# FFN weights in two halves, the residual loaded into place, VectorE memsets: one change to an S4 and GEGLU kernel, predicted and measured

## The chip, the cores and the metric

The kernel runs on one core of one Trainium2 chip. The metric is the device time of one execution in microseconds (us). "Faster" or "slower" needs 2%. The intervals are 95% intervals of the ratio to the kernel before, measured in the same rounds on the same chip.

Engine names as in the profile: PE is TensorE (PEld its weight loads), DVE is VectorE, ACT is ScalarE, POOL is GpSimd, SP is SyncE. "SPq" and "ACTq" are transfers issued by those engines, and an engine works through its instructions in order. The granted clock of a stretch is the share of TensorE's full clock that the throttle allowed in it. L90 is line 90 of the kernel; the change moves line numbers by a few, so L708 before and L705 after are the same statement.

## The reference, cut to what matters

```python
# u: [1, 2048, 448] bf16; N = 256 states per channel; F = 1792
K = einsum("dn,dnl,dn->dl", C, exp(dt * A * l), dt * B).real       # S4 convolution kernel
y = irfft(rfft(pad(K)) * rfft(pad(layernorm(x))))[:L] + layernorm(x) * Dskip
h  = x + y                                                          # x is the residual
h2 = h + (gelu(ln(h) @ w_gate) * (ln(h) @ w_up)) @ w_down           # the FFN
# outputs: h2 and the gradients of h2 for all twelve inputs (vjp with grad_out)
```

## The kernel before

One core computes forward and backward. These stages matter here, in order of time: the kernel K is generated and its lags are expanded (`expand_lags`, to 393 us); K is transformed (`dft_forward`, to 452); the product is transformed back and becomes h (`dft_inverse`, to 530); the FFN forward and backward (550 to 829); the transform of the gradient (to 892); a second inverse for dK (to 946); the binning of dK into lags (`bin_lags`, to 978); a third inverse for the input's gradient (to 1038); a last phase over the states.

Names in the code and the profiles: a slice is one pass `kt` of the loop below, and the variants (var) are sums, negatives and differences of input tiles that its matmuls read. Kh, Kx and Kperm are K as loaded, reordered and expanded, and pxl is the expansion's PSUM tile. Uk is a slice of the input's spectrum, xn the normalised input, hn the normalised h, goT the transposed output gradient. Rb and blo are the one-hot and the result tiles of the binning, Mn and Mb the lag tables, DY what the third inverse transforms. A ring is a set of buffers used in turn.

The forward transform, with its variants all built at the start:

```python
var = [work.tile([P, 3, D], BF16, name="var%d" % i) for i in range(8)]
for rho in range(4):
    for jj in range(2):
        s1, s2 = sig[4 * rho + jj], sig[4 * rho + jj + 2]
        nc.vector.tensor_tensor(out=V(rho, jj, 0), in0=s1, in1=s2, op=ALU.add)
        nc.scalar.mul(out=V(rho, jj, 2), in_=s2, mul=-1.0)
for rho in range(4):
    for jj in range(2):
        nc.vector.tensor_tensor(out=V(rho, jj, 1), ..., op=ALU.subtract)
# ... (mid rows)
for kt in range(8):
    # 4 groups of matmuls into PSUM tiles pgrp (a ring of 7)
    on_kt(kt, groups)       # VectorE: butterflies into X, product with Uk into Z[kt]
```

After it, the weights and then the residual, all on SyncE's queue:

```python
self.ffn_weights()          # Wg, Wu (8 loads), WdT (4 transposes), Wd, WgT and WuT (28 transposes)

def consume(tp, pp, pm, scale):            # per tile of the inverse
    x = tmp.tile([P, D], BF16, name="x_t")
    xn = tmp.tile([P, D], BF16, name="xn_t")
    nc.sync.dma_start(out=x[:], in_=tok_rows_ap(self.aps["A_u"][0], tp))
    nc.sync.dma_start(out=xn[:], in_=self.xn_dram[:, tp, :])
    # xn *= Dskip; x += xn; y from PSUM; h_sb[:, tp] = x + y
```

The lag tables and the binning:

```python
nc.gpsimd.memset(self.Mn[:], 0.0)                    # rs_open: 128 x 11200 bf16
nc.gpsimd.memset(t[:], 0.0)                          # Mb, twice 128 x 3200
# bin_lags, for b in range(6): one-hot tiles Rb on VectorE, matmuls into pbl,
# blo[:, 0] by VectorE and blo[:, 1] by ScalarE (a ring of two buffers), then
self.dq().dma_start(out=self.dKl_dram[:][...], in_=o[0:n, :, :])
# rs_load: 40 loads Mn <- dKl_scr, three of four on SyncE, the fourth on ScalarE
```

## Time and profile before

| | us |
|---|---|
| time, median of 3 runs (range) | 1419.27 (1416.28 to 1423.09) |
| span of the profiled run | 1417.6 |
| Kperm complete (end of the expansion) | 393.5 |
| last product of the kernel transform | 451.6 |
| end of the first inverse | 529.6 |
| gate matmuls (ps_g) at full rate | 549.8 |
| end of the second inverse; first DY matmul of the third | 945.7; 977.6 |

The averages of the whole span say little here. In the profile TensorE and VectorE are busy 76% and 79% of the time, but in different stages. The useful question for each stage is which wait ends last in it.

### The profile page before, as it was taken

How to read it: one execution, taken by the hardware profiler on the slowest of the kernel's cores; microseconds unless marked ns; L12 is line 12 of the kernel's file. 1: busy time of each engine (PE TensorE's matmuls, PEld its weight loads, DVE VectorE, ACT ScalarE, POOL GpSimd, SP SyncE). 2: the span in 40 equal slices, each digit the busy share in tenths (PEclk: the TensorE clock that was granted, in tenths of full speed). 3: DMA queues.
4: the chain of work that ended last, by engine and by line, in shares of the span. 5: the costliest groups of instructions: out<-in, count | busy, mean ns of one | idle time of the engine just before them, and what ended most of it. 6: DMA issues, size and time to landing. Idle time of an engine off the chain costs nothing.

```text
span 1417.6 us, 21047 instructions
## 1 busy us (share of the span) xinstructions
PE 1082.5 (76%) x7284; PEld 684.3 (48%) x7284; DVE 1120.4 (79%) x2999; ACT 643.5 (45%) x1110; POOL 275.0 (19%) x378
## 2 busy tenths in 40 slices
PE   0363677877786746999999977877969899779874
PEld 0143355555343325776777633433436555566553
DVE  5889879778798047999999969975796786686785
ACT  3574776858431014665666631111425634552450
POOL 2933544010101000111111120031110221220221
PEclk9855566767998978999999989897989999979986
DMA  5033243343664742344443272225359977988940
GB/s 143 33 134 124 77 181 154 135 163 119 229 216 154 166 117 56 100 114 112 114 113 100 85 242 72 79 56 128 111 126 192 223 165 163 192 176 191 211 82 6
DMA packets 320120, 189.76 MB, mean 134 GB/s; under 512 B 268809, under 2 KB 291661, under 8 KB 319885
## 3 DMA queue, kind: packets, MB, share of 16 engines
q1 hardware_dynamic: 302224, 143.50, 39.1%
q0 software_dynamic: 13696, 42.45, 9.5%
q10 hardware_dynamic: 4092, 2.47, 0.7%
q8 instruction: 57, 0.93, 0.3%
q14 instruction: 51, 0.41, 0.1%
HBM read 44.98 MB, written 83.22 MB: 90 GB/s over the span
## 4 chain that ended last, share of the span: by engine, by line
PE 30%; DVE 19%; DMA 8%; issue 6%; SPq 5%; ACT 3%; POOL 1%; ACTq 0%; DVEq 0%; POOLq 0%
PE ps_o L90 7%; PE pinv L90 5%; PE pw L90 3%; DMA TTr<-T_scr 3%; DMA out_dram<-emit_o 3%; PE pim L1225 3%; PE pre L1225 3%; PE ps_g L90 2%; PE ps_u L90 2%; PE ps_d L90 2%; PE pc L1205 2%; DVE e_t L826 1%; SPq L796 1%; SPq L797 1%; PE pgrp L90 1%
## 5 line engine op out<-in xcount | busy, mean ns | idle before, releaser
L90 PE MATMUL pw<-rowsT,act_b 128*128 128x512 bf16 (+1 forms) x512 | 125.4, 363 | 2.4 <-DMA rowsT<-dG_scr 1.7
L1183 DVE TENSOR_TENSOR u<-C,tb_Z 128x1280 bf16<-128x1280 bf16 x140 | 104.5, 819 | 22.1 <-ACT C L1208 20.8
L1208 ACT CAST C<-pc 128x400 bf16<-128x400 f32 x224 | 102.5, 493 | 39.4 <-PE pc L1205 37.6
L90 PE MATMUL kb<-Pt,T 128*128 128x50 bf16 x896 | 86.0, 264 | 22.5 <-DVE Pt L470 16.6
L90 PEld LDWEIGHTS <-TS 128*128 128x128 bf16 x576 | 57.2, 99 | 92.3 <-issue 42.5
L1205 PE MATMUL pc<-Mb,TTr 128*128 128x100 bf16 x896 | 86.2, 226 | 19.8 <-DMA TTr<-T_scr 8.1
L90 PEld LDWEIGHTS <-TC 128*128 128x128 bf16 x576 | 57.6, 100 | 88.2 <-issue 39.2
L1205 PEld LDWEIGHTS <-TTr 128*128 128x128 bf16 x896 | 66.6, 108 | 68.6 <-issue 42.3
L90 PEld LDWEIGHTS <-T 128*128 128x128 bf16 x896 | 79.5, 122 | 37.5 <-issue 21.3
L606 PE MATMUL pa<-Rq,hl_a 128*128 128x256 bf16 x224 | 43.6, 338 | 59.9 <-DVE Rq L586 46.3
L606 PE MATMUL pa<-Rq,hl_b 128*128 128x256 bf16 x224 | 50.9, 370 | 47.6 <-ACT Cs L648 45.7
L647 ACT ACTIVATE Sn<-pa 128x1024 bf16<-128x1024 f32 x56 | 57.5, 1026 | 49.1 <-DVE T L652 34.8
L90 PEld LDWEIGHTS <-act_b 128*128 128x128 bf16 x512 | 49.4, 100 | 38.6 <-issue 7.6
L90 PE MATMUL ps_d<-goT,WdT 128*128 128x256 bf16 x448 | 61.7, 281 | 6.7 <-DVE ln_v L250 4.7
L606 PEld LDWEIGHTS <-hl_a 128*128 128x128 bf16 x224 | 26.2, 118 | 82.2 <-issue 49.7
L90 PE MATMUL pinv<-Zf,TS 128*128 128x448 bf16 x128 | 45.0, 373 | 26.5 <-DVE ybf L767 26.5
L90 PE MATMUL ps_g<-hnT,Wg 128*128 128x256 bf16 x448 | 60.0, 277 | 6.2 <-DMA hnT<-hn_scr 6.0
L648 ACT ACTIVATE Cs<-pa,halfpi_col 128x1024 bf16<-128x1024 f32 x56 | 62.5, 1117 | 3.0 <-DVE T L653 2.8
L90 PE MATMUL ps_u<-hnT,Wu 128*128 128x256 bf16 x448 | 60.5, 278 | 2.9 <-ACT e_up L864 2.9
L606 PEld LDWEIGHTS <-hl_b 128*128 128x128 bf16 x224 | 27.2, 125 | 72.1 <-issue 64.0
L1225 PEld LDWEIGHTS <-ident 128*128 128x128 bf16 x525 | 52.3, 100 | 18.6 <-issue 7.5
L1256 POOL DMA_DIRECT2D out_dram<-emit_o x84 | 43.9, 529 | 75.9 <-ACT emit_o L1254 72.1
(297 smaller groups left out, 2962.8 us busy)
## 6 DMA issues: line engine op xcount, KB each, us to landing
T_scr<-T SPq DMA_DIRECT2D x56, 512.0 KB
Uk<-U_scr SPq DMA_DIRECT2D x16, 448.0 KB
aT_scr<-f_a POOLq DMA_DIRECT2D x8, 896.0 KB, 6.2
dG_scr<-f_dG POOLq DMA_DIRECT2D x8, 896.0 KB, 7.9
dU_scr<-f_dU POOLq DMA_DIRECT2D x8, 896.0 KB, 9.9
TC<-tab_scr SPq DMA_DIRECT2D x16, 256.0 KB
TS<-tab_scr SPq DMA_DIRECT2D x16, 256.0 KB
U_scr<-X SPq DMA_DIRECT2D x8, 448.0 KB
```

The costliest lines, as they stand in the source:

```text
L90: self.nc.tensor.matmul(out_ap, lhsT=lhsT, rhs=rhs, start=(i == 0), stop=(i == n - 1))
L606: nc.tensor.matmul(pa[:, 2 * h:2 * h + 2, nh, :], lhsT=self.hl[nm][:, blk, nh * 128:(nh + 1) * 128], rhs=Rqf[:, c0:c0 + 256].rearrange("p ...
L647: nc.scalar.activation(out=flat(Sn), in_=flat(pb), func=ACT.Sin)
L648: nc.scalar.activation(out=flat(Cs), in_=flat(pb), func=ACT.Sin, bias=self.halfpi_col[:], scale=-1.0)
L796: nc.sync.dma_start_transpose(out=WgT[:, ft, :], in_=aps["B_w_gate"][:, ft * P:(ft + 1) * P])
L797: nc.sync.dma_start_transpose(out=WuT[:, ft, :], in_=aps["B_w_up"][:, ft * P:(ft + 1) * P])
L826: TT = lambda o, x, y, op: nc.vector.tensor_tensor(out=o[:], in0=x[:], in1=y[:], op=op)
L1183: TT = lambda o, x, y, op: nc.vector.tensor_tensor(out=o, in0=x, in1=y, op=op)
L1205: nc.tensor.matmul(pc[:, k, :, :].rearrange("p r x -> p (r x)"), lhsT=tt[:, k0 + k, c, nh, :], rhs=mv[:, t0 + k0 + k, :], start=True, stop ...
L1208: nc.scalar.copy(out=C[:, c, :, nh, x0:x0 + 8].rearrange("n x (m r) -> n x m r", r=2), in_=pc[:].rearrange("n m r x -> n x m r"))
L1225: nc.tensor.matmul(dst[:], lhsT=wt[:], rhs=prods[i][:, o, :, :].rearrange("p w n -> p (w n)"), start=(o0 == 0 and o == 0 and i in (0, 2)), ...
L1256: nc.gpsimd.dma_start(out=outs[idx][blk * 64:(blk + 1) * 64, nh * P:(nh + 1) * P], in_=ob[nh * 64:(nh + 1) * 64, :])
```

## The change

Its intent is to let the first inverse run without waiting. One half of the weights is loaded during the kernel transform. The residual goes straight into its final tile h_sb, early and on another queue. To make room in SBUF the variants of the transform are built in three groups, two buffers deep, and the ring of Uk and X has two buffers instead of three. In the lag binning GpSimd is freed of its memsets.

```diff
-            var = [work.tile([P, 3, D], ...)]                       # all variants at the start
+            for kts, which in (((0, 1), 0), ((2, 3, 6, 7), 2), ((4, 5), 1)):
+                var = [work.tile([P, D], BF16, name="var%d" % i) for i in range(8)]   # bufs=2
+                ...                                                 # build this group's variants only
+                for kt in kts: ...
@@ forward_conv
+            for tp in range(NT):
+                nc.scalar.dma_start(out=self.h_sb[:, tp, :], in_=tok_rows_ap(self.aps["A_u"][0], tp))
+            self.ffn_open()
...
-                ring = ...(name="fc_ring2", bufs=3)
+                ring = ...(name="fc_ring2", bufs=2)
...
+                    if kt in (2, 3, 4):
+                        self.ffn_weights_first(kt - 2)              # Wg, Wu, WdT
...
-            self.ffn_weights()
+            self.ffn_weights_rest()                                 # Wd, WgT, WuT
             def consume(tp, pp, pm, scale):
-                x = tmp.tile(...); nc.sync.dma_start(out=x[:], ...)
+                x = self.h_sb[:, tp, :]
-                nc.sync.dma_start(out=xn[:], in_=self.xn_dram[:, tp, :])
+                nc.scalar.dma_start(out=xn[:], in_=self.xn_dram[:, tp, :])
@@ bin_lags, rs_open, rs_load
-                self.dq().dma_start(out=self.dKl_dram...)
+                nc.gpsimd.dma_start(out=self.dKl_dram...)
-        nc.gpsimd.memset(self.Mn[:], 0.0)            # and Mb
+        nc.vector.memset(self.Mn[:], 0.0)            # and Mb
-                self.dq(alt=True).dma_start(out=tab, in_=src)
+                (nc.gpsimd if k % 2 else nc.scalar).dma_start(out=tab, in_=src)
```

(The tiles Kh and lag_t of the expansion move to smaller rings; the weight loads are the same but for their order.)

More of the change, by code (lines that the diff above doesn't have):

```diff
@@ L123, in dft_forward @@
         with ExitStack() as es:
-            work = es.enter_context(self.tc.tile_pool(name="dftf_work", bufs=1))
+            work = es.enter_context(self.tc.tile_pool(name="dftf_work", bufs=2))
             psA = es.enter_context(self.tc.tile_pool(name="dftf_psA", bufs=7, space=bass.MemoryType.PSUM))
             psB = es.enter_context(self.tc.tile_pool(name="dftf_psB", bufs=1, space=bass.MemoryType.PSUM))
-            var = [work.tile([P, 3, D], BF16, name="var%d" % i) for i in range(8)]
-            def V(rho, jj, which):
-                return var[2 * rho + jj][:, which, :]
@@ L132, in dft_forward @@
-            for rho in range(4):
-                for jj in range(2):
-                    s1 = sig[4 * rho + jj]
-                    s2 = sig[4 * rho + jj + 2]
-                    nc.vector.tensor_tensor(out=V(rho, jj, 0), in0=s1, in1=s2, op=ALU.add)
-                    nc.scalar.mul(out=V(rho, jj, 2), in_=s2, mul=-1.0)
-            for rho in range(4):
-                for jj in range(2):
-                    nc.vector.tensor_tensor(out=V(rho, jj, 1), in0=sig[4 * rho + jj], in1=sig[4 * rho + jj + 2], op=ALU.subtract)
@@ L142, in dft_forward @@
-            for comp, (rp, rn) in enumerate(((0, 2), (1, 3))):
-                pm = psB.tile([P, D], F32, name="pmid")
-                self.mm_group(pm[:], [(self.ones[:], V(rp, jj, 0)) for jj in range(2)]
-                              + [(self.neg_ones[:], V(rn, jj, 0)) for jj in range(2)])
-                nc.scalar.copy(out=mid[:, comp, :], in_=pm[0:1, :])
-            for kt in range(8):
-                groups = {}
-                for comp in (0, 1):
-                    for par in (0, 1):
-                        pairs = self.dft_pairs(kt, comp, par, self.TC[kt], self.TS[kt], sig, V)
-                        pt = psA.tile([P, D], F32, name="pgrp")
-                        self.mm_group(pt[:], pairs)
-                        groups[(par, comp)] = pt
-                on_kt(kt, groups)
+            for kts, which in (((0, 1), 0), ((2, 3, 6, 7), 2), ((4, 5), 1)):
+                var = [work.tile([P, D], BF16, name="var%d" % i) for i in range(8)]
+                for rho in range(4):
+                    for jj in range(2):
+                        v = var[2 * rho + jj]
+                        s1, s2 = sig[4 * rho + jj], sig[4 * rho + jj + 2]
+                        if which == 2:
+                            nc.scalar.mul(out=v[:], in_=s2, mul=-1.0)
+                        else:
+                            nc.vector.tensor_tensor(out=v[:], in0=s1, in1=s2, op=ALU.add if which == 0 else ALU.subtract)
+                if which == 0:
+                    for comp, (rp, rn) in enumerate(((0, 2), (1, 3))):
+                        pm = psB.tile([P, D], F32, name="pmid")
+                        self.mm_group(pm[:], [(self.ones[:], var[2 * rp + jj][:]) for jj in range(2)]
+                                      + [(self.neg_ones[:], var[2 * rn + jj][:]) for jj in range(2)])
+                        nc.scalar.copy(out=mid[:, comp, :], in_=pm[0:1, :])
+                for kt in kts:
+                    groups = {}
+                    for comp in (0, 1):
+                        for par in (0, 1):
+                            pairs = self.dft_pairs(kt, comp, par, self.TC[kt], self.TS[kt], sig, lambda rho, jj, w: var[2 * rho + jj][:])
+                            pt = psA.tile([P, D], F32, name="pgrp")
+                            self.mm_group(pt[:], pairs)
+                            groups[(par, comp)] = pt
+                    on_kt(kt, groups)
@@ L687, in expand_lags @@
             lag_row = w.tile([P, NT, P], BF16, name="lag_row")
-            t = w.tile([P, 4, 4, P], F32, name="lag_t")
-            nc.gpsimd.iota(t[:], pattern=[[1, 4], [512, 4], [4, P]], base=0, channel_multiplier=0,
-                           allow_small_or_imprecise_dtypes=True)
-            nc.vector.tensor_copy(out=lag_row[:], in_=t[:].rearrange("p r j l -> p (r j) l"))
+            for r in range(4):
+                t = rp.tile([P, 4, P], F32, name="lag_t", bufs=2)
+                nc.gpsimd.iota(t[:], pattern=[[512, 4], [4, P]], base=r, channel_multiplier=0,
+                               allow_small_or_imprecise_dtypes=True)
+                nc.vector.tensor_copy(out=lag_row[:, 4 * r:4 * r + 4, :], in_=t[:])
             Kx = w.tile([P, 6, D], BF16, name="Kx")
-            Kh = w.tile([P, 6, D], BF16, name="Kh")
-            nc.gpsimd.memset(Kh[:, 5, :], 0.0)
             for b in range(6):
                 n = 1 if b == 5 else P
-                self.dq().dma_start(out=Kh[0:n, b, :], in_=Kt_dram[:][b * 128:b * 128 + n, :])
-                nc.scalar.copy(out=Kx[:, b, :].rearrange("p (x r) -> p x r", r=2), in_=Kh[:, b, :].rearrange("p (r x) -> p x r", r=2))
+                Kh = rp.tile([P, D], BF16, name="Kh", bufs=3)
+                if b == 5:
+                    nc.gpsimd.memset(Kh[:], 0.0)
+                self.dq().dma_start(out=Kh[0:n, :], in_=Kt_dram[:][b * 128:b * 128 + n, :])
+                nc.scalar.copy(out=Kx[:, b, :].rearrange("p (x r) -> p x r", r=2), in_=Kh[:].rearrange("p (r x) -> p x r", r=2))
             for tp in range(NT):
@@ L732, in forward_conv @@
             tmp = es.enter_context(self.tc.tile_pool(name="fc_tmp", bufs=3, side="right"))
+            for tp in range(NT):
+                nc.scalar.dma_start(out=self.h_sb[:, tp, :], in_=tok_rows_ap(self.aps["A_u"][0], tp))
+            self.ffn_open()
             with ExitStack() as el:
                 kp = el.enter_context(self.tc.tile_pool(name="fc_kperm", bufs=1))
-                ring = el.enter_context(self.tc.tile_pool(name="fc_ring2", bufs=3))
-                pf = el.enter_context(self.tc.tile_pool(name="fc_pf", bufs=2))
+                ring = el.enter_context(self.tc.tile_pool(name="fc_ring2", bufs=2))
                 Kperm = kp.tile([P, NT, D], BF16, name="Kperm")
                 self.expand_lags(Kt_dram, Kperm)
+                pf = el.enter_context(self.tc.tile_pool(name="fc_pf", bufs=2))
                 def on_k(kt, groups):
@@ L748, in on_k @@
                         self.prod_mid(self.Umid, self.Kmid, rows, False, pf)
+                    if kt in (2, 3, 4):
+                        self.ffn_weights_first(kt - 2)
                 self.dft_forward([Kperm[:, t, :] for t in range(NT)], self.Kmid, on_k)
-            self.ffn_weights()
+            self.ffn_weights_rest()
             def consume(tp, pp, pm, scale):
-                x = tmp.tile([P, D], BF16, name="x_t")
+                x = self.h_sb[:, tp, :]
                 xn = tmp.tile([P, D], BF16, name="xn_t")
-                nc.sync.dma_start(out=x[:], in_=tok_rows_ap(self.aps["A_u"][0], tp))
-                nc.sync.dma_start(out=xn[:], in_=self.xn_dram[:, tp, :])
+                nc.scalar.dma_start(out=xn[:], in_=self.xn_dram[:, tp, :])
                 nc.vector.tensor_tensor(out=xn[:], in0=xn[:], in1=self.dsk_row[:], op=ALU.mult)
-                nc.vector.tensor_tensor(out=x[:], in0=xn[:], in1=x[:], op=ALU.add)
+                nc.vector.tensor_tensor(out=x, in0=xn[:], in1=x, op=ALU.add)
                 y = tmp.tile([P, D], BF16, name="ybf")
@@ L767, in consume @@
                     nc.vector.scalar_tensor_tensor(out=y[:], in0=pm[:], scalar=-scale, in1=t[:], op0=ALU.mult, op1=ALU.add)
-                nc.vector.tensor_tensor(out=self.h_sb[:, tp, :], in0=x[:], in1=y[:], op=ALU.add)
+                nc.vector.tensor_tensor(out=x, in0=x, in1=y[:], op=ALU.add)
             self.dft_inverse(Z, rows, consume)
@@ L773, with ffn_open, ffn_weights_first, ffn_weights_rest @@
     GELU_C1 = math.sqrt(2.0 / math.pi)
-    def ffn_weights(self):
+    def ffn_open(self):
+        self.w_stack = ExitStack()
+        self.ff_wp = wp = self.w_stack.enter_context(self.tc.tile_pool(name="ff_w", bufs=1))
+        NCT = len(self.CT)
+        self.Wg = wp.tile([P, NCT, self.F], BF16, name="Wg")
+        self.Wu = wp.tile([P, NCT, self.F], BF16, name="Wu")
+        self.WdT = wp.tile([P, NCT, self.F], BF16, name="WdT")
+    def ffn_weights_first(self, i):
+        nc = self.nc
+        W = (self.Wg, self.Wu, self.WdT)[i]
+        for ct, (c0, ps) in enumerate(self.CTT):
+            if i < 2:
+                nc.sync.dma_start(out=W[ps, ct, :], in_=self.aps["B_w_gate" if i == 0 else "B_w_up"][c0:c0 + P, :][ps, :])
+            else:
+                nc.sync.dma_start_transpose(out=W[:, ct, :], in_=self.aps["B_w_down"][:, c0:c0 + P])
+        nc.gpsimd.memset(W[0:64, len(self.CT) - 1, :], 0.0)
+    def ffn_weights_rest(self):
         nc = self.nc
         D, F, NFT = self.D, self.F, self.NFT
-        NCT = len(self.CT)
         aps = self.aps
-        self.w_stack = ExitStack()
-        wp = self.w_stack.enter_context(self.tc.tile_pool(name="ff_w", bufs=1))
-        Wg = wp.tile([P, NCT, F], BF16, name="Wg")
-        Wu = wp.tile([P, NCT, F], BF16, name="Wu")
-        WdT = wp.tile([P, NCT, F], BF16, name="WdT")
+        wp = self.w_stack.enter_context(self.tc.tile_pool(name="ff_w2", bufs=1))
         Wd = wp.tile([P, NFT, D], BF16, name="Wd")
@@ L788, in ffn_weights @@
         rstd2 = wp.tile([P, NT], F32, name="rstd2")
-        for ct, (c0, ps) in enumerate(self.CTT):
-            nc.sync.dma_start(out=Wg[ps, ct, :], in_=aps["B_w_gate"][c0:c0 + P, :][ps, :])
-            nc.sync.dma_start(out=Wu[ps, ct, :], in_=aps["B_w_up"][c0:c0 + P, :][ps, :])
-        for ct, (c0, _) in enumerate(self.CTT):
-            nc.sync.dma_start_transpose(out=WdT[:, ct, :], in_=aps["B_w_down"][:, c0:c0 + P])
         nc.sync.dma_start(out=Wd[:], in_=aps["B_w_down"].rearrange("(t p) d -> p t d", p=P))
@@ L797, in ffn_weights @@
             nc.sync.dma_start_transpose(out=WuT[:, ft, :], in_=aps["B_w_up"][:, ft * P:(ft + 1) * P])
-        for W in (Wg, Wu, WdT):
-            nc.gpsimd.memset(W[0:64, NCT - 1, :], 0.0)
-        self.ffw = (Wg, Wu, Wd, WgT, WuT, WdT, rstd2)
+        self.ffw = (self.Wg, self.Wu, Wd, WgT, WuT, self.WdT, rstd2)
     def ffn(self):
@@ L1139, in bin_lags @@
                 nc.scalar.activation(out=ov[:, 1], in_=pv, func=ACT.Copy, scale=self.val_col[0:n, b:b + 1])
-                self.dq().dma_start(out=self.dKl_dram[:][b * P:b * P + n, :, :], in_=o[0:n, :, :])
+                nc.gpsimd.dma_start(out=self.dKl_dram[:][b * P:b * P + n, :, :], in_=o[0:n, :, :])
     def rs_open(self):
@@ L1151, in rs_open @@
             t = big.tile([P, MM, 2, 2 * NO], BF16, name="Mb%d" % i)
-            nc.gpsimd.memset(t[:], 0.0)
+            nc.vector.memset(t[:], 0.0)
             self.Mb.append(t)
@@ L1159, in rs_load @@
     def rs_load(self):
+        nc = self.nc
+        k = 0
         for w in range(2):
             for tab, src in self.lag_dmas(self.Mn[:, :, w, :], self.dKl_dram[:, w, :]):
-                self.dq(alt=True).dma_start(out=tab, in_=src)
+                k += 1
+                (nc.gpsimd if k % 2 else nc.scalar).dma_start(out=tab, in_=src)
     def rs_phase(self):
```

## The prediction

> **What bounds the kernel now.** I read the waits first, then the chain that ended last, then a window table by stage. The waits (engine, line, what ended the wait; total, count, longest in us) give one event of about 48 us seen by three engines:
>
> ```profile
> DVE x_t L760 <- DMA x_t<-in_A_u_dram: 48.5, 2, 48.3
> ACT evtmp L766 <- DVE ybf L767: 29.1, 1, 29.1
> PE pinv L90 <- DVE ybf L767: 26.5, 1, 26.5
> ```
>
> VectorE waited 48.3 us for the first residual tile x_t, and when the buffers behind it filled, TensorE stood still for 26.5 us. The chain (start, length, who) says why the tile was late: SyncE's queue works in order, and all FFN weights stand ahead of x_t in it.
>
> ```profile
> 456.08 7.39 SPq L793
> ...
> 505.38 1.25 SPq L797
> 506.68 1.25 SPq L796
> 507.98 1.25 SPq L797
> 509.34 2.15 DMA x_t<-in_A_u_dram
> 513.14 16.46 PE pinv L90 x76
> ...
> 892.40 53.35 PE pinv L90 x272
> ```
>
> L793 is the four WdT transposes (456.1 to 471.3 in the full chain), L796/L797 the 28 WgT/WuT transposes, one per 1.30 us. The last line is the same inverse transform with nothing in its way: 272 matmuls in 53.35 us. The first one runs from 446.8 to 529.3, 82.5 us. So about 29 us are the queue's fault. Which engine bounds the neighbours is in the windows (stretch, length; busy us of PE, PEld, DVE, ACT, POOL; granted clock, DMA share, GB/s):
>
> ```profile
> 380.00:393.00 13.00, 9.39 (x40) 3.84 (x39) 11.45 (x39) 7.21 (x15) 0.00 (x0) 0.98 0.93 293
> 393.00:403.00 10.00, 9.55 (x51) 4.83 (x51) 9.99 (x27) 7.11 (x16) 0.56 (x1) 1.00 0.98 357
> 403.00:446.00 43.00, 29.16 (x151) 14.53 (x149) 43.00 (x83) 7.18 (x13) 3.24 (x6) 0.91 0.36 121
> 471.00:509.00 38.00, 15.67 (x83) 8.02 (x82) 0.00 (x0) 1.26 (x3) 1.58 (x1) 0.75 0.55 133
> ```
>
> In the kernel transform (403 to 446) VectorE is busy 43.00 of 43.00 us: anything added to it there lengthens the stage. Before it (380 to 403) the DMA engines are 93 to 98% busy: transfers added there slow others. Last, the timeline of the lag binning:
>
> ```profile
> 946.64 12.66 DVE L1130 TENSOR_SCALAR Rb<-val_row,lag_col 128x128 bf16<-128x128 bf16 x6
> 946.93 9.51 POOL L1148 MEMSET Mn<- 128x11200 bf16 x1
> 956.38 5.70 POOL L1152 MEMSET Mb<- 128x3200 bf16 x2
> 957.67 4.49 DVE L1130 TENSOR_SCALAR Rb<-val_row,lag_col 128x128 bf16<-128x128 bf16 x4
> 977.62 0.53 PE L90 MATMUL pinv<-DY,TC 128*128 128x448 bf16 x1 [4.27 <-ACT blo L1139]
> 977.88 16.62 SPq L1162 DMA_DIRECT2D Mn<-dKl_scr  x26
> ```
>
> Six Rb tiles take 12.66 us and four take 4.49 us (0.25 to 0.27 us each elsewhere in the trace), just while GpSimd clears Mn and Mb. The third inverse (DY) starts only at 977.62.
>
> **What the Trainium skill says.** (1) "SBUF — State Buffer", section "SBUF: two separate sides": VectorE in its two-port modes and GpSimd share a port pair under an exclusive lock, held for a whole instruction. The trace agrees: 12.66 us for six Rb against 9.51 us of memset plus six times 0.26. (2) "VectorE: DVE Perf Modes", section "Zero memsets can be issued as uint32 (trn2)": one cycle per element whatever the type, and a zero memset over bf16 can go out as 4-byte words; its Specifications give 0.96 GHz. In the trace a VectorE memset of 64 words took 112 ns and one of 128 bf16 took 165 ns, 53 ns for 64 elements, which is near it. (3) "DMA: Bandwidth & Descriptors", section "Issuing engines are not separate DMA queues": another issuing engine saves only issue time, the 16 DMA engines are shared. The share of 0.98 at 357 GB/s agrees that moving early loads to ScalarE's queue doesn't get them out of the way.
>
> **The change part by part.**
>
> *Kernel expansion (380 to 393).* The 16 residual loads (1.8 MB) go on ScalarE's queue. In its instruction order they lie between the third-last and last Kx copies, so those copies wait for all 16 issues (about 0.4 us each, and DMA completion slots are reused every eight, so later ones also wait for earlier transfers, U_scr and the first Wg load among them, in the busiest DMA stretch of the kernel). Before, the Kx copies ended at 383.9; I put the last ones at about 390.5. Half of the pxl matmuls need them; some slack exists, so the stage ends about 7 us later (range 4 to 10): **+7**.
>
> *Forward transform of the kernel.* The variants are now built in three groups. Eight subtractions (2.5 us for eight at 395.4) move from the start, where VectorE mostly waited for the first matmul group, into the stage where it is 100% busy; the freed start gives little back. Some residual additions also slip in. Slices 6 and 7 are made before 4 and 5, so the inverse that follows waits about 1 us longer for slice 5: **+2.7** together. End of the last product: 451.65 + 7 + 2.7, about 461.
>
> *First inverse.* The second weight half is now Wd, 28 transposes of 1.3 us (36.7) and about 10 us of goT transposes, on a queue that no consumer stands in: the residual is in its final tile and xn_t comes by ScalarE's queue. So the inverse runs like its twin, and ends about 51 us after the last product: 461 + 51 = 512, against 529.7: **-17** net of the 9.7 above. The rest of the weights needs 47 us beside it and should just be done.
>
> *FFN start.* Before, hn_scr's write waited behind eight goT transposes:
>
> ```profile
> 531.21 10.11 SPq L842 DMA_TRANSPOSE goT<-go_scr  x8
> 541.43 0.52 SPq L837 DMA_DIRECT2D hn_scr<-hn  x1
> ```
>
> hn was ready at 536.8; the write could go then, 541.4 - 536.8 = 4.6 us earlier, since the goT transposes now run during the inverse: **-4.6**. The FFN itself (TensorE busy 275.8 of 280 us) is untouched.
>
> *Forward transform of the output gradient (838 to 892).* The same regrouping, no new loads: **+3**.
>
> *Lag binning (946 to 978).* The VectorE memsets are 5600 + 2 x 1600 words, 8800 / 0.96 GHz = 9.2 us (estimate from the skill's rate). They stand on VectorE ahead of most Rb tiles, so the 9.5 us Mn block is swapped, not removed. What goes is the Mb contention (4.49 - 1.05 = 3.4 us) less its share on VectorE (3.3), which by itself is nothing; the real gain is that the dKl writes now leave on GpSimd's queue instead of behind rowsT transposes of 4.0, 4.5 and 4.8 us on SyncE, and that Mn issues (4.58 us for two) no longer hold ScalarE ahead of the last blo, for which TensorE waited 4.27 us: **-5** (range -9 to -2).
>
> *Third inverse (978 to 1043).* 26 Mn loads held SyncE's queue for 16.62 us ahead of xn_t, VectorE waited 3.20 us for it. They are now on GpSimd and ScalarE, 20 each; ScalarE issues them at 0.4 to 0.65 us ahead of its normalisation work: **-2**. Nothing after that changes.
>
> Sum: -17 - 4.6 + 3 - 5 - 2 = -25.6 us. 1419.3 - 25.6 = **1393.7**; I round to 1393.
>
> **The rivals.** (a) *The early loads give more back than 7 us.* 380 to 403 is at 293 to 357 GB/s already; 1.8 MB more at 357 GB/s is 5 us of pure transfer, and the first Wg, Wu and WdT loads stand in SyncE's queue ahead of the third spectrum tile Uk, whose ring shrinks from three to two buffers. If Uk comes late VectorE waits, and that goes straight into the span: 10 us more, total about 1404. For it: the DMA shares. Against it: 121 GB/s from 403 on, so room to catch up. (b) *The memsets only change engines.* VectorE has 9.2 us more to do at the point where GpSimd blocked it 9.5 us, and ScalarE's 20 Mn issues hold its normalisation: lag binning and third inverse gain 0 instead of 7, total about 1400. For it: VectorE's Rb make the path there. Against it: the late dKl writes show directly in the chain. (c) *Everything overlaps better.* If the Kx copies cost only 2 us and binning gains 10: about 1382. For it: the pxl matmuls waited less than half the time for Kx before. (d) *The inverse meets another wait*, such as xn_t issued by a ScalarE busy with evacuations; its twin with similar evacuations ran at 53.35, so I give this little.
>
> **Range and chances.** The inverse gain, before what is given back, is 27 to 29 us and sure; the errors are those of the expansion (about 5 us), the binning (4), the rest (4), together some 8 us as root of squares, times 1.3 for 8 in 10, and a longer tail up: 1393, range 1378 to 1409. The 2% line is 1419.3 x 0.98 = 1390.9, two us below my value: faster by over 2%: 0.43, within: 0.55, slower: 0.02.
>
> **What would show it.** Right: no wait of VectorE at L760, the 272 pinv of the first inverse in 51 to 54 us, the first full-rate ps_g about 20 us after the inverse's end becomes 15; the last Kx copy near 390 and Kperm complete near 400; VectorE's subtractions inside the transform; memset Mn about 5.8 us on VectorE and Rb at 0.26 us; DY's first pinv about 5 us sooner after the second inverse. Wrong: if Kx copies end before 385, the +7 falls and the kernel is over 2% faster; if VectorE shows waits for Uk of over 3 us in the transform, rival (a); if the time from the second inverse's end to DY's first pinv stays at 32 us, rival (b).

## The result, and the profile after

The changed kernel takes **1395.77 us** (median of 4 runs, 1394.3 to 1396.96). The ratio to the kernel before is 0.9833, interval [0.9807, 0.9859], so by the 2% rule it is the same. A ratio is the mean time of one kernel's fast runs over that of the other's of the same rounds, so it is not quite the ratio of the medians quoted.

The total is 2.8 us from the prediction. The stages are not so close. This table is worked out from the two traces, each row from the event above it to its own:

| stage | before | after | difference | predicted |
|---|---|---|---|---|
| start to Kperm complete | 393.5 | 405.9 | +12.4 | +7 |
| to the last product of the kernel transform | 58.1 | 64.6 | +6.5 | +2.7 |
| to the end of the first inverse | 78.0 | 49.6 | -28.4 | -27 |
| to ps_g at full rate | 20.2 | 15.5 | -4.7 | -4.6 |
| FFN, to its last matmul | 279.2 | 276.8 | -2.4 | 0 |
| to the gradient transform's first matmul into pgrp | 9.6 | 6.8 | -2.8 | in the next row |
| to the second matmul of the second inverse | 54.1 | 60.0 | +5.9 | +3 |
| rest of the second inverse | 53.0 | 54.0 | +1.0 | 0 |
| to DY's first matmul (binning) | 31.9 | 23.4 | -8.5 | -5 |
| third inverse | 60.3 | 60.6 | +0.3 | -2 |
| rest | 379.7 | 375.3 | -4.4 | 0 |

The waits on x_t and TensorE's 26.5 us wait in the first inverse are gone. In the chain after the change (start, length, who) the inverse is one unbroken piece:

```profile
465.77 54.38 PE pinv L90 x272
```

It takes 54.38 us; its twin, the second inverse, takes 54.34 in this trace. The timeline of SyncE's queue, and TensorE's first gate matmuls at full rate, show the FFN's start:

```profile
461.05 10.16 SPq L850 DMA_TRANSPOSE goT<-go_scr  x8
527.30 0.39 SPq L845 DMA_DIRECT2D hn_scr<-hn  x1
535.60 1.22 PE L90 MATMUL ps_g<-hnT,Wg 128*128 128x256 bf16 x5 [0.87 <-DMA hnT<-hn_scr]
```

The goT transposes now run at the start of the inverse instead of after it, and hn_scr's write goes 7.2 us after the inverse's end (520.1) instead of 11.8 us. So far the change does what it was meant to do.

The price is in the expansion. Before the change the last four Kx copies followed one another on ScalarE:

```profile
381.72 2.16 ACT L698 COPY Kx<-Kh 128x448 bf16<-128x448 bf16 x4
```

After it:

```profile
380.67 1.13 ACT L695 COPY Kx<-Kh 128x448 bf16<-128x448 bf16 x2
381.64 11.93 ACTq L731 DMA_DIRECT2D h_sb<-in_A_u_dram  x16
393.62 1.64 ACT L695 COPY Kx<-Kh 128x448 bf16<-128x448 bf16 x3 [11.82 <-DMA TC<-tab_scr]
```

Sixteen issues hold ScalarE for 11.93 us, and the last three Kx copies stand behind them. They end at 395.3 instead of 383.9. The issues themselves add up to 6.4 us, 0.4 each. In the other 5.6 us the next issue waited for an earlier transfer to land (the input's spectrum, or residual tiles issued before). The waits between 376 and 472 us say what followed (engine, what ended the wait; total, count, longest):

```profile
PE pgrp L90 <- DVE var L136: 13.6, 3, 12.0
PE pxl L90 <- ACT Kx L695: 12.1, 1, 12.1
ACT Kx L695 <- DMA TC<-tab_scr: 11.8, 1, 11.8
DVE xn_t L760 <- DMA xn_t<-xn_scr: 2.6, 1, 2.6
```

TensorE waited 12.1 us for Kx. Early in the transform VectorE waited 2.6 us for one xn_t tile: five of the residual's additions now stand in this stage in VectorE's order, before the change one did. Later TensorE waited 12.0 us at once for the third group of variants. The windows there (stretch, length; busy PE, PEld, DVE, ACT, POOL; clock, DMA share, GB/s):

```profile
420.00:446.00 26.00, 17.97 (x96) 9.10 (x93) 26.00 (x50) 4.26 (x8) 3.70 (x5) 0.90 0.79 229
446.00:452.00 6.00, 1.08 (x2) 0.23 (x3) 6.00 (x13) 0.00 (x0) 0.54 (x1) 0.50 0.41 141
```

VectorE is busy throughout, while TensorE does 1.08 us of work in 6 us and its granted clock falls to 0.50. TensorE is not the bound here. But after 452 VectorE needs what TensorE has not yet made: it waits 1.2 and 1.0 us for petmp and pgrp.

In the binning the timeline shows the memsets in their new place:

```profile
935.17 4.72 DVE L1156 MEMSET Mn<- 128x5600 uint32 x1 [1.09 <-issue]
940.17 1.39 DVE L1160 MEMSET Mb<- 128x1600 uint32 x1 [0.28 <-issue]
943.50 6.07 PE L90 MATMUL pbl<-dKt,Rb 128*128 128x448 bf16 x16 [8.93 <-DVE Rb L1138]
956.59 0.53 PE L90 MATMUL pinv<-DY,TC 128*128 128x448 bf16 x1 [2.48 <-ACT blo L1147]
```

The row of the Mn memset shows 4.72 us on VectorE, against 9.51 us on GpSimd before. But VectorE also stood idle ahead of each memset with no wait that the profile names, and that time grows with the memset: 0.28 us for 1600 words, 0.39 for 2240 (in the run with shared-out clearing), 1.09 for 5600. So it is counted with the memset here: 5.81 us for Mn and 1.67 for each Mb, 9.15 in all, from 934.08 to 943.24. TensorE still waits 8.93 us for an Rb tile behind it.

### The profile page after: what moved, and what is told of

The parts are those of the page before. It is cut to its first block, busy times and chain, and to the rows that moved or that the text cites. A ratio compares the mean times of both kernels' runs of the same rounds, so it can differ in the third digit from the quotient of the medians.

```text
span 1392.5 us, 21021 instructions
## 1 busy us (share of the span) xinstructions
PE 1077.7 (77%) x7264; PEld 681.9 (49%) x7284; DVE 1116.7 (80%) x3005; ACT 642.4 (46%) x1110; POOL 275.9 (20%) x404
## 4 chain that ended last, share of the span: by engine, by line
PE 31%; DVE 15%; DMA 9%; issue 9%; ACT 2%; POOL 2%; SPq 0%; POOLq 0%; ACTq 0%; DVEq 0%
PE pinv L90 8%; PE ps_o L90 6%; DMA TTr<-T_scr 4%; PE pw L90 3%; DMA out_dram<-emit_o 3%; PE pgrp L90 3%; PE pim L1236 3%; PE pre L1236 2%; DVE e_t L834 2%; PE ps_u L90 2%; PE ps_g L90 2%; PE ps_d L90 2%; PE pc L1216 1%; DVE e_gl L834 1%; DVE f_dG L886 1%
## 5 line engine op out<-in xcount | busy, mean ns | idle before, releaser
L90 PE MATMUL pw<-rowsT,act_b 128*128 128x512 bf16 (+1 forms) x492 | 121.3, 362 | 7.4 <-DVE dskout L1065 2.7
L90 PEld LDWEIGHTS <-T 128*128 128x128 bf16 x896 | 79.7, 123 | 37.5 <-issue 21.3
L643 ACT ACTIVATE Cs<-pa,halfpi_col 128x1024 bf16<-128x1024 f32 x56 | 62.5, 1116 | 3.0 <-DVE T L648 2.8
L1267 POOL DMA_DIRECT2D out_dram<-emit_o x84 | 44.5, 535 | 73.3 <-ACT emit_o L1265 60.3
L873 ACT ACTIVATE e_hp<-e_w 128x512 bf16<-128x512 bf16 x56 | 35.4, 632 | 50.8 <-DVE e_w L834 50.1
L90 PE MATMUL ps_d<-goT,WdT 128*128 128x256 bf16 x448 | 58.1, 273 | 0.8 <-DVE ybf L768 0.8
```

The lines of the kernel that those rows point to most:

```text
L90: self.nc.tensor.matmul(out_ap, lhsT=lhsT, rhs=rhs, start=(i == 0), stop=(i == n - 1))
L643: nc.scalar.activation(out=flat(Cs), in_=flat(pb), func=ACT.Sin, bias=self.halfpi_col[:], scale=-1.0)
L873: nc.scalar.activation(out=hp[:], in_=w[:], func=ACT.Sigmoid, scale=2.0 * c1g)
L1267: nc.gpsimd.dma_start(out=outs[idx][blk * 64:(blk + 1) * 64, nh * P:(nh + 1) * P], in_=ob[nh * 64:(nh + 1) * 64, :])
```

## The experiments

Twelve kernels ran, each with 3 timed rounds (4 runs). Unless said otherwise each is the changed kernel with one edit. For the time, compare the ratio to the kernel before with the changed kernel's 0.9833, since the runs of different calls were on different chips. Stage times come from one trace each.

How much such a single trace scatters can be told from stages whose code is the same. The time from the third inverse's end to the end of the run lay between 375.3 and 384.7 us in the fourteen traces. The kernel transform with unchanged code took 64.6, 63.8, 64.1 and 64.3 us in four traces. It took 68.0 and 68.6 us in two others, where VectorE also waited for Kf_scr writes before it could reuse the two-deep ring. In the six traces that leave both stages as changed, DY started 23.4 to 25.2 us after the second inverse, and the third inverse took 60.1 to 61.0 us. So a stage difference of 4 us in one trace is not evidence by itself.

### Late residual loads

```diff
-            for tp in range(NT):
-                nc.scalar.dma_start(out=self.h_sb[:, tp, :], in_=...)
...
+            for tp in range(NT):                      # after the transform, ahead of ffn_weights_rest
+                nc.sync.dma_start(out=self.h_sb[:, tp, :], in_=...)
             self.ffn_weights_rest()
```

> The changed kernel with one edit: the 16 residual loads go on SyncE's queue after the last spectrum tiles, so they are neither in ScalarE's order ahead of the Kx copies nor in the DMA traffic of 380 to 405 us. Theory (the loads cost the expansion stage its 12.4 us, Kperm complete at 405.9 instead of 393.5): the last Kx copy ends near 384 to 386, Kperm is complete by 397 at the latest, and the time falls by 7 to 12 us, to 1384 to 1389 us. Rival (the first weight loads and the tables delay the stage, the residual loads only share the wait): Kperm complete at 402 or later, time 1393 to 1397 us.

Measured: 1384.25 us (1381.36 to 1387.4), ratio 0.9739 [0.9714, 0.9763], which is faster by the 2% rule. The last Kx copy ended at 387.9 us and Kperm was complete at 396.8. The kernel transform also fell, from 64.6 to 61.0 us. So the early loads cost some 9 us of the 12.4 in the expansion and 3.6 more behind it. The theory's time and its Kperm hold; the last Kx copy is later than its 384 to 386. What is left, 3.4 us over the kernel before, has another candidate: the Kh tiles now have a ring of three buffers. Before, their six loads were all issued by 380.2 us; here the last three go at 380.5, 382.9 and 385.0. No run isolates this. The inverse kept its 49.3 us, so the residual did not need to be early; it only must not stand behind the weights.

### Early loads on GpSimd's queue

```diff
-                nc.scalar.dma_start(out=self.h_sb[:, tp, :], in_=...)
+                nc.gpsimd.dma_start(out=self.h_sb[:, tp, :], in_=...)
```

> The changed kernel with one edit: the 16 residual loads stay as early as they are, but GpSimd's queue issues them instead of ScalarE's. It parts the two ways in which the loads could delay the Kx copies. Theory A (the order on ScalarE's queue: copies stand behind 16 issues that wait for transfers): the last Kx copy ends by 388 and Kperm is complete by 398, like the late loads, time 1384 to 1389 us. Theory B (their 1.8 MB of traffic while the DMA engines are 95% busy delays the tables and Kh): Kperm complete at 402 or later, time over 1392 us.

Measured: 1407.96 us (1406.68 to 1411.43), ratio 0.9909 [0.9887, 0.993]; the last Kx copy at 413.9, Kperm at 416.4. By its numbers this is theory B, but the trace shows a wait that neither theory had. Three lines of the timeline:

```profile
392.20 1.79 POOL L731 DMA_DIRECT2D h_sb<-in_A_u_dram  x3 [0.28 <-DMA h_sb<-in_A_u_dram]
393.98 0.49 POOL L693 MEMSET Kh<- 128x448 bf16 x1
413.32 0.61 ACT L695 COPY Kx<-Kh 128x448 bf16<-128x448 bf16 x1 [4.59 <-DVE xn_t L760]
```

The memset of the last Kh tile is on GpSimd, and now it stood behind the sixteen issues. Its load could go only at 406.7, behind the tables on SyncE. ScalarE then issued four xn_t loads (408.3 to 413.2), which stood ahead of the last Kx copy, and this followed at 413.3. The run is inconclusive between A and B. It shows the same kind of loss on a second queue.

### Small loads at the early place

```diff
-                nc.scalar.dma_start(out=self.h_sb[:, tp, :], in_=tok_rows_ap(...))
+                nc.scalar.dma_start(out=self.h_sb[:, tp, 0:32], in_=tok_rows_ap(...)[:, 0:32])
...
+            for tp in range(NT):                      # the full loads, late
+                nc.sync.dma_start(out=self.h_sb[:, tp, :], in_=...)
```

> The changed kernel with one edit: at their early place on ScalarE's queue the 16 residual loads move only 32 of 448 columns each (0.13 of 1.8 MB); the full loads follow late on SyncE's queue, as in the run with late loads (there: last Kx copy at 387.9 us, Kperm complete at 396.8, against 395.3 and 405.9 in the changed kernel). It keeps the order on ScalarE's queue and its waits for completion slots, and takes the early traffic away. Theory A (order and slots: the copies stand behind 16 issues which wait for other transfers): last Kx copy at 392 or later, Kperm complete at 401 or later, time 1391 to 1396 us. Theory B (the 1.8 MB of traffic): last Kx copy by 389, Kperm by 398, time 1383 to 1388 us.

Measured: 1393.18 us (1391.44 to 1395.77), ratio 0.9798 [0.9778, 0.9817]; the last Kx copy at 395.0, Kperm at 404.7. The timeline of ScalarE:

```profile
383.07 10.25 ACTq L731 DMA_DIRECT2D h_sb<-in_A_u_dram  x16
393.37 1.64 ACT L695 COPY Kx<-Kh 128x448 bf16<-128x448 bf16 x3 [10.13 <-DMA h_sb<-in_A_u_dram]
```

With 7% of the bytes the issues still held ScalarE for 10.25 us, 6.2 of it in the issues and 4.0 (instead of 5.6) in waits between them. The DMA engines' share of busy time from 384 to 392 us fell from 0.99 and 1.00 to 0.74 and 0.88. This decides for theory A: **the expansion's loss is the order on ScalarE's queue, not the bytes of these loads.** The kernel transform behind it fell to 61.1 us, as with the late loads. The traces name most of those 3.5 us: in both runs VectorE's wait for xn_t in the transform (2.6 us) is gone, and one residual addition and one product with Dskip fewer (0.8 us) fall into the stage. The early residual alone does not do it: with the weight split undone (below) the residual is early, there is no such wait, and the transform took 61.6 us. Where early residual and early weights come together, six of seven traces have the wait (1.5 to 2.8 us).

### The third group of variants earlier

```diff
-            for kts, which in (((0, 1), 0), ((2, 3, 6, 7), 2), ((4, 5), 1)):
+            v0 = build(0); ...; one(0, v0); one(1, v0)
+            v2 = build(2); one(2, v2); one(3, v2)
+            v1 = build(1)                             # was: after slice 7
+            one(6, v2); one(7, v2); one(4, v1); one(5, v1)
```

> The changed kernel with one edit: VectorE builds the third group of variants (the eight subtractions) after slice 3 instead of after slice 7; same instructions, other place, in both forward transforms. Theory (a bubble: TensorE stood 12 us waiting for these variants, and afterwards VectorE, which bounds the stage, had nothing to work on until TensorE had refilled): the stage from Kperm complete to the last product falls from 64.6 to 60 to 62 us and the gradient's from 60.0 to 56 to 58, the whole by 5 to 9 us, to 1387 to 1391 us. Rival (the subtractions cost only their own 2.5 us of VectorE each time, wherever they stand): no change, 1394 to 1398 us.

Measured: 1392.19 us (1387.71 to 1393.67), ratio 0.9797 [0.9776, 0.9819]. The kernel transform took 61.9 us (64.6), the gradient's 56.3 (60.0). TensorE's wait for variants in this stage:

```profile
PE pgrp L90 <- DVE var L136: 2.2, 2, 1.6
```

It was 13.6 us in the changed kernel. The stages are as the theory had them; the time is just above its range. The intervals of the ratios just overlap, so the total gain of about 5 us (0.0036 x 1419) is likely rather than proved.

### The grouping alone, on the kernel before

The edit replaces `dft_forward` in the kernel before by the changed kernel's; nothing else.

> The kernel before with one part of the change alone: the variants built in three groups, slices in the order 0 1 2 3 6 7 4 5. Theory (the grouping by itself lengthens both forward transforms, by a bubble of TensorE and VectorE at the third group): from Kperm complete to the last product 60 to 63 us instead of 58.1, the gradient's transform 57 to 60 instead of 54.1 with 2 to 3 us given back ahead of it, time 3 to 7 us over the kernel before of the same rounds. Rival (it is the two-deep ring, the early weights and the residual additions that lengthen the kernel transform): within 2 us of the kernel before.

Measured: 1428.86 us (1428.08 to 1431.11) against 1421.44, ratio 1.0053 [1.0025, 1.0081]. The kernel transform took 61.3 us (58.1) and the gradient's 59.2 (54.1), and nothing was given back ahead of it (10.2 instead of 9.6). So the grouping alone costs 3.2 and 5.1 us, about 7.5 us in total, slightly more than expected.

### The weight split undone

```diff
-            self.ffn_open()                           # ahead of the expansion
-                    if kt in (2, 3, 4): self.ffn_weights_first(kt - 2)
+            self.ffn_open()                           # after the transform
+            for i in range(3): self.ffn_weights_first(i)
             self.ffn_weights_rest()
```

> The changed kernel with the split of the weights undone: Wg, Wu and WdT are loaded after the kernel transform again, with the rest, while the residual still comes on its own. Theory (the split matters because the whole weight load, about 57 us on SyncE's queue plus 10 us of goT transposes, outlasts the 50 us inverse): the inverse still ends 49 to 51 us after the last product, but the time from its end to the full-rate gate matmuls grows from 15.5 to 23 to 30 us, less up to 4 us won in the expansion; time 1399 to 1408 us. Rival (taking the residual out of the weight queue was all that counted, the rest is hidden anyway): that stage stays at 15 to 17 us, time 1390 to 1397 us.

Measured: 1409.47 us (1407.53 to 1414.18), ratio 0.9906 [0.9884, 0.9929]. The inverse took 49.4 us after the last product, and from its end to ps_g at full rate 21.3 us instead of 15.5, between theory and rival. SyncE's queue shows why it grew:

```profile
536.66 1.25 SPq L808 DMA_TRANSPOSE WuT<-in_B_w_up_dram  x1
538.02 0.52 SPq L845 DMA_DIRECT2D hn_scr<-hn  x1
```

The inverse had ended at 525.3, but hn_scr's write went only after the last weight transpose. In the changed kernel that last transpose ends at 515.5, 4.6 us before the inverse. So the split is worth about 6 us here, and the 28 us of the inverse come from the residual and xn no longer standing behind the weights. The rest of this run's loss is a side effect: the goT transposes moved ahead of the tables on SyncE, ScalarE's sixteen issues took 16.69 us, and Kperm was complete only at 414.3.

### The memsets back on GpSimd

```diff
-        nc.vector.memset(self.Mn[:], 0.0)             # and Mb
+        nc.gpsimd.memset(self.Mn[:], 0.0)
```

> The changed kernel with one edit: Mn and Mb are cleared by GpSimd again; dKl writes and Mn loads stay on their new queues. From the end of the second inverse to DY's first matmul the kernel before took 31.9 us, the changed one 23.4. Theory (the memsets are most of it, 15.2 us on GpSimd with VectorE locked against 7.5 us on VectorE): 29 to 33 us and a time of 1401 to 1405 us. Rival (the queues are most of it): 23 to 27 us, time 1396 to 1399 us.

Measured: 1408.13 us (1406.23 to 1408.67), ratio 0.9904 [0.9886, 0.9922]. DY started 28.2 us after the second inverse (23.4 in the changed kernel, 31.9 before). That is just below the theory's range and above the rival's. So the memsets are worth 4.7 of the 8.5 us; the lock is back in the trace:

```profile
936.59 12.64 DVE L1138 TENSOR_SCALAR Rb<-val_row,lag_col 128x128 bf16<-128x128 bf16 x6
936.79 9.58 POOL L1156 MEMSET Mn<- 128x11200 bf16 x1
```

The third inverse grew too, from 60.6 to 65.6 us, which nobody expected. In it ScalarE's nb_u waited 20.1 us for Mn issues and VectorE up to 12.4 us for nb_u. Binning and third inverse together took 92.2 us before, 84.1 in the changed kernel and 93.8 here, so over both stages the whole gain is gone with the memsets. The kernel transform of this trace is one of the two slow ones (68.0 us), so not all of the 10 us that the ratio shows need belong to the edit.

### The dKl writes back on SyncE's queue

```diff
-                nc.gpsimd.dma_start(out=self.dKl_dram..., ...)
+                self.dq().dma_start(out=self.dKl_dram..., ...)
```

> The changed kernel with one edit: the dKl writes go back to SyncE's queue, behind the rowsT transposes; memsets and Mn loads as changed. With the memsets put back instead, the time from the end of the second inverse to DY's first matmul grew from 23.4 to 28.2 us, of 31.9 in the kernel before; 3.7 us are left for the queues. Theory (they are the dKl writes' queue): 26 to 29 us. Rival (they are the Mn issues, taken off ScalarE ahead of the last blo): 23 to 25 us. Time 1396 to 1401 us.

Measured: 1402.0 us (1399.53 to 1403.46), ratio 0.986 [0.9831, 0.9888]; DY started 24.0 us after the second inverse. The writes' queue is worth 0.5 us here, within the scatter of the stage. But the third inverse took 63.4 us instead of 60.6, which was not expected; both stages together are 3.3 us longer, and the ratio shows 4 us. A candidate for the remaining 3 us of the binning are the Mn issues, which no longer stand ahead of the last blo on ScalarE: TensorE's wait for that blo fell from 4.27 to 2.48 us. No run isolates it, so it is not shown.

### The clearing shared out

```diff
-        nc.vector.memset(self.Mn[:], 0.0)
+        nc.scalar.mul(out=self.Mn[:, 0:15], in_=<a column, broadcast>, mul=0.0)
+        nc.vector.memset(self.Mn[:, 15:], 0.0)
...                                                    # Mb cleared in rs_load
```

> The changed kernel with the clearing of the lag tables shared out: ScalarE, idle for 13 us there, writes 60% of Mn as zero times a column, VectorE clears the rest of Mn, and Mb after the lag binning. Theory (the 7.5 us of VectorE memsets ahead of the Rb tiles are on the path: TensorE waits 8.9 us for an Rb): end of the second inverse to DY's first matmul from 23.4 to 17 to 19 us, time 1389 to 1392 us. Rival (the Mn table itself, or ScalarE's blo behind its long write, then sets the end): 22 us or more, time 1394 to 1398 us.

Measured: 1399.26 us (1394.67 to 1402.45), ratio 0.9837 [0.9811, 0.9862]; DY started 23.3 us after the second inverse. This is the rival's result, through another wait than it named. The second batch of Rb tiles began at 936.9 instead of 943.2 us, yet nothing was gained at the end. The two Mb memsets, meant to follow the binning, still ran inside it (at 937.9 and 941.5). A VectorE line of the timeline:

```profile
950.69 0.62 DVE L1146 CAST blo<-pbl 128x448 bf16<-128x448 f32 x1 [3.30 <-DMA dKl_scr<-blo]
```

VectorE waited for a dKl write to land before it could reuse one of the two blo buffers.

### The same with six blo buffers

```diff
-            op = ...(name="bl_o", bufs=2)
+            op = ...(name="bl_o", bufs=6)
```

> The run with shared-out clearing, plus six blo buffers instead of two. There the clearing no longer held the first Rb tiles (943.2 became 936.9 us), yet DY started no sooner (23.3 us): VectorE waited up to 3.3 us for a dKl write before it could reuse a blo buffer. Theory (that wait took the memset's place): 17 to 20 us from the second inverse to DY, time 1389 to 1393 us. Rival (the matmuls of the binning or ScalarE set the end): 22 us or more, no gain.

Measured: DY started 19.6 us after the second inverse, so that wait had indeed taken the memset's place. The time did not follow: 1399.58 us (1396.19 to 1402.33), ratio 0.9851 [0.9817, 0.9885]. The third inverse took 62.5 us instead of 60.6, and its waits name the next in line:

```profile
ACT nb_u L269 <- DMA Mn<-dKl_scr: 20.1, 1, 20.1
DVE nb_v L271 <- ACT nb_u L269: 11.2, 2, 10.8
```

Half of what the binning won was lost again one stage later. The other half is within the scatter of the runs.

### All Mn loads on GpSimd's queue

```diff
-                (nc.gpsimd if k % 2 else nc.scalar).dma_start(out=tab, in_=src)
+                nc.gpsimd.dma_start(out=tab, in_=src)
```

> The changed kernel with all 40 Mn loads on GpSimd's queue instead of 20 there and 20 on ScalarE's. Theory (the Mn issues hold ScalarE's normalisation: nb_u waits 17.9 us for them and VectorE 8.9 us for nb_u, which costs the third inverse what xn_t gained): the third inverse from 60.6 to 56 to 58 us, time 1391 to 1394 us. Rival (those waits lie beside TensorE, or the dx writes behind 40 loads take their place): 60 us or more, no change, 1394 to 1399 us.

Measured: 1403.45 us (1399.53 to 1406.91), ratio 0.9868 [0.9842, 0.9894]; the third inverse took 59.7 us. The nb_u wait on Mn issues was gone, the gain 0.9 us. That is near the rival's 60 us and far from the theory's 56 to 58: with the loads as they are in the changed kernel, those waits cost little. VectorE waited 4.5 us for xn_t in their place. By the ratio this run is 5 us slower than the changed kernel, outside both ranges. Its trace is the other one with a slow kernel transform (68.6 us), and it has the longest last phase (384.7); no cause is shown.

### All of it together

The edits are the late residual loads, the third group after slice 3, and the shared clearing with six blo buffers.

> All that the experiments point to in one kernel: late residual loads on SyncE's queue, the third group of variants built after slice 3, shared-out clearing with six blo buffers. If the three parts add up (11.5 for the loads, 3 to 5 for the variants, 3 to 6 for the binning), 1373 to 1381 us; if the binning gains nothing, 1379 to 1383 us.

Measured: **1376.41 us** (1374.12 to 1382.95), ratio 0.9689 [0.9654, 0.9724]. It is faster than the kernel before by 3.1% and than the changed kernel by about 1.5% (0.9689 / 0.9833 = 0.985). The kernel transform took 58.8 us, the gradient's 57.7, DY started after 20.4 us and the third inverse took 62.1. The late loads and the earlier variants carry the gain: alone they brought 13 and 5 us by their ratios, together with the clearing 20, and binning and third inverse are only 1.6 us shorter than in the changed kernel.

## Why the prediction was right or wrong

The time: 1395.8 for 1393.0, right. The sum was right partly by luck, because errors cancelled: with the two gradient rows taken together, the terms that were too favourable miss by 12.6 us and those that were too cautious by 11.8. And the range (1378 to 1409) is wider than its own working: 8 us times 1.3 is 10 us to each side.

- **The inverse without the queue** (51 us after the last product): right, 49.6. Taking the residual out from behind the weights did it; with the split undone the inverse is as short. That the remaining weights would "just be done" is right too: they end 4.6 us before the inverse.
- **FFN start, -4.6**: right, -4.7, by the mechanism given (hn_scr's write behind the goT transposes).
- **Kernel expansion, +7 (range 4 to 10)**: right mechanism, wrong size: +12.4. I took the last Kx copies to be at 390.5; they ended at 395.3. The sixteen issues alone took 6.4 us, as estimated at 0.4 each; the term that was too small is the waits between them, 5.6 us. The small loads show that it is the queue's order, with some 1.5 us of these waits from the loads' own bytes, so rival (a) explains little of this stage. The prediction has no term for the ring of Kh, which may be behind the 3.4 us that stay with the late loads.
- **Kernel transform, +2.7**: too small, +6.5. The grouping by itself is 3.2 (the run of the grouping alone). I counted the subtractions' own time and the late slice 5, but not the bubble (a stretch in which an engine has nothing to do): TensorE idle for 12.0 us, then VectorE short of work. The other 3.5 us came with the early loads: mostly a wait of VectorE for xn_t, which rival (d) named for the inverse, and not the late Uk tiles of rival (a).
- **Gradient transform, +3**: +5.9 with 2.8 less ahead of it, so +3.1 together. The sum looks right, but for the grouping I was wrong: alone it costs 5.1 us there and gives nothing back. The 2.8 us ahead are not explained; one visible difference is a VectorE tile operation (nb_c) beside a GpSimd memset, 2.08 us before and 0.56 after.
- **Lag binning, -5**: more was won, -8.5, and not where the working put it. The estimate of the memsets was right: 9.2 us, measured 9.15 with the idle time ahead of their rows. (The rows alone give 7.5 us; the 53 ns for 64 elements in the prediction is the same rate of the rows, 0.83 ns per element.) The step "the 9.5 us Mn block is swapped, not removed" failed by a double count: the 9.2 us already hold Mb's 3.3, which the next sentence charges again. The prediction's own figures give 9.5 + 3.4 - 9.2 = 3.7 us won; putting the memsets back costs 4.7. The step "the real gain is that the dKl writes now leave on GpSimd's queue" failed: 0.5 us in this stage. Rival (b), no gain, is wrong here.
- **Third inverse, -2**: nothing came of it (+0.3). The xn_t wait fell from 3.20 to 0.32 us, but nb_u waited 17.9 us for Mn issues on ScalarE, as the working feared. Moving those issues away brought 0.9 us, while an xn_t wait of 4.5 us came back; what bounds this stage is not shown.
- **Nothing else changes**: the FFN was 2.4 us shorter. The traces of all kernels with the whole change have it (276.5 to 276.8), the grouping alone has not (279.1); I have no cause. The last phase's -4.4 us is within the scatter of that stage and should not be explained.

What stays open: whether the 3 us left in the binning are the Mn issues; whether the 3.4 us left in the expansion are the ring of Kh; why the third inverse grew when the dKl writes went back; the cause of the FFN's 2.4 us; and the third inverse's growth when the binning is shortened, where the Mn issues are named by the waits but not shown as the cause.

## What to carry to other kernels

An early load on the queue of an engine that also computes is not free: its issues stand in that engine's order and can wait for other transfers, so put it where nothing urgent stands behind it, and no earlier than needed. When you split preparatory work to save memory, place each piece at least one step ahead of its use: TensorE had slack, and the bubble still reached the engine that was the bound. After removing a wait, look for the next buffer or queue in line before counting the gain; here a ring of two blo buffers took a memset's place. And when a row of the profile looks too short for its work, look at the idle time just before it.

## What the Trainium skill lacked or had wrong

- "VectorE: DVE Perf Modes", Specifications and "Zero memsets can be issued as uint32 (trn2)": the rate stated there, one cycle per element at 0.96 GHz, holds here, but the section does not say that a memset's row in the profile reads short. The rows give (4.72 - 1.39) / 4000 = 0.83 ns per word; with the idle time ahead of them the memsets of 1600, 2240 and 5600 words took 1.67, 2.32 and 5.81 us, where the page's rate gives 1.67, 2.33 and 5.83.
- "DMA: Bandwidth & Descriptors", "Issuing engines are not separate DMA queues": it says that issuing on several engines only saves sequencer time. It gives no figure for how long a run of issues, and the waits between them, can hold the issuing engine's own computation. The runs show ScalarE held for 11.93 us by sixteen issues (6.4 us of issues, 5.6 of waits), and for 10.25 us when they moved 7% of the bytes.
- No page consulted gives a scatter for one trace's stages. Here the same code took 375.3 to 384.7 us in the last phase, and 63.8 to 68.6 us in the kernel transform.
